# A fused attention, MLP and top-1 mixture-of-experts kernel: routing from raw products, tau loaded elsewhere, and a new order of work around the first expert

## The chip, the cores and the metric

The kernel runs on one core of a Trainium2 chip. The metric is the device time of one execution in microseconds (us); the lower, the better. Engines are named as in the profile: PE is TensorE (PEld its weight loads), DVE is VectorE, ACT is ScalarE, POOL is GpSimd, SP is SyncE, which here only issues DMAs.

## The reference

Three stages run one after the other; the output of each is the input of the next.

```
# attention: batch 4, 8 heads, 576 positions, head size 64, window of 64
scores = where(0 <= i - j < 64, scale * q @ k.T, -1e9)
x = softmax(scores) @ v                       # -> 2304 tokens x 512
# MLP: 512 -> 2048 -> 512
h = x @ w_in;  y = max(0.01 * h, h) @ w_out
# top-1 of 8 experts, 512 -> 1024 -> 512
yn = y / (norm(y) + 1e-6);  en = emb / (norm(emb) + 1e-6)
logits = yn @ en.T / tau
e = argmax(logits);  p = exp(logits - max(logits))
gate = p[e] / (sum(p) + 1e-9)
out = gate * (relu(y @ w1[e]) @ w2[e])
```

## The kernel before

Everything is held in 32-bit floats; the matrix products of the MLP and of the experts are done with each operand split into a high and a low part (three products each), so that every weight tile and every activation tile is first cast to its high part (ACT, sometimes DVE) and then has its low part computed by a subtraction (DVE or POOL).

**Attention** (the first 230 us) goes through 36 chunks of queries. For each, PE transposes q and k (`pq`, `pk`), forms scores `pS` (L344), DVE takes their maximum `mx` (L355), ACT the exponential `sm` (L358), DVE or POOL scales it (`su`, L360 to L362), PE transposes it (`pt`, L380) and multiplies by v (`po`, L396), and ACT and DVE split the result into `xT` (L407, L412). Between these chunks run the first products of the MLP, and the MLP's weights, which come as 64-bit numbers, are turned into 32-bit ones: these conversion pieces are `cv_a` (L189, L190) and `cv_u` (L192, L194) on DVE, L187 and L196 on ACT, L197 on POOL or DVE.

**The MLP** runs in three passes over 16 slices of the hidden layer (4, 4 and 8). A step is a first product `ph` (L537), the leaky ReLU `hs` (ACT L544, DVE L545), its split `gh` (ACT L549, POOL L550), and the second product `acc` (L564), which DVE adds into `ypart` (L575). In the last pass each block of tokens is routed as soon as it is complete (`route`).

**Routing** writes the block's rows to `y_dram`, forms the dot products with the eight normalised expert vectors (on DVE, L654, or for the last two blocks on PE: `py`, `pl`), and the squares of the rows (ACT L643). `sqrt_into` takes the square root by three Newton steps on DVE (L97 to L105), L684 to L686 scale the products by the norm and by tau (`rt`), L688 to L696 find the expert as a one-hot row (`ohf`, `ohb`), L702 to L707 compute the gate. PE counts ranks (`pp<-ohb`, L715), DVE turns them into list positions (`di`, L722 to L730), and POOL scatters token numbers and gates into `list_dram` (L733). Routing is a generator; each `yield "w"` hands control back to the step list of PE.

**The experts.** The expert with the most tokens so far is taken first (`choose_first`), its weights and a first list `ixte` are loaded early, and its tokens are gathered (`prep1`, L899) and transposed (`prep2`, `px` L910, `x2f` L913). The first pair of 128-token tiles (`pair`) computes `ph` (L980) for eight slices: the first four side by side in 48 matmuls, then the rest one after the other, evacuated to `xT` by ACT L983 and DVE L984; then `po` (L956). Work of the last block's routing, the sorting of experts by size (`sort_experts`, L825 to L832), the counting registers (`count_registers`, L842 to L859, result `cnt_i`), the list of the first expert (`load_idx(0, ...)`, L884) and the remaining splits of its weights (`early_split`, L785 high, L786 low) are hung between these matmuls as hooks: hook 0 to 3 after each 12 of the first 48 matmuls, hook 4 after the first two evacuations, hook 5 to 8 after each further slice, and from there after the second products. At hooks 12 to 16 the engines load the counts (`TENSOR_LOAD cnt_i`).

**Order.** On PE everything runs in program order. On DVE, ACT, POOL and SP a scheduler orders the work by priority until the first expert is chosen; from there on their order is the program's too. The conversion pieces have a priority lowered by 100 places, several pieces of the attention a raised one; what stands where in the queues follows from all of these together.

## Time and profile before

| | |
|---|---|
| median of 3 runs | 852.87 us (850.72 to 853.14) |
| profiled execution, its own time | 854.09 us |
| its span in the trace | 852.5 us |
| PE busy | 797.0 us, 93% of the span |
| DVE busy | 541.8 us, 64% |
| ACT busy | 400.4 us, 47% |
| POOL busy | 309.1 us, 36% |
| mean granted clock of PE | 0.984 |

The span is what the trace shows from the first to the last instruction; 1.6 us of the execution's own time lie around it. A busy share is the time in which an engine had an instruction running. The granted clock is the TensorE clock that the chip allowed, as a fraction of the full 2.4 GHz; 0.5 is 1.2 GHz.

### The profile page before, as it was taken

To read this page: it belongs to the slowest core of one execution; us is meant where nothing else is said; L and a number is where in the kernel's file an instruction comes from. 1 tells how busy PE (TensorE), PEld (TensorE's weight loads), DVE (VectorE), ACT (ScalarE), POOL (GpSimd) and SP (SyncE) were. 2 spreads that over 40 slices of the span, in tenths; PEclk is the share of its full clock that TensorE was granted. 3 is DMA by queue.
4 is the path that set the end of the run, shared out by engine and by line. 5 is a ranking of instruction groups with operands and counts; after the bars stand their busy time and mean duration, and the time that the engine had idled before them with its cause. 6 is when DMAs were issued, how large, how long until landed. Compare 5 with 4: busy or idle time off the path is not lost.

```text
span 852.5 us, 13946 instructions
## 1 busy us (share of the span) xinstructions
PE 797.0 (93%) x4864; PEld 712.4 (84%) x4864; DVE 541.8 (64%) x1272; ACT 400.4 (47%) x971; POOL 309.1 (36%) x300
## 2 busy tenths in 40 slices
PE   8688888999999999999999998987899999999994
PEld 6677787888898999999988887876789989889893
DVE  5999698976468222827798899847251166363560
ACT  5787668867554222523323233353342255454551
POOL 2354332232343232342333443452552145244431
PEclk9899999999999999999999999999899999999998
DMA  9668555852256443232203212073681147385610
GB/s 223 173 155 203 115 154 151 231 143 69 60 186 180 124 149 109 90 115 95 89 24 87 51 38 75 27 233 117 200 271 38 38 154 254 142 275 174 210 63 18
DMA packets 101189, 113.01 MB, mean 133 GB/s; under 512 B 61662, under 2 KB 80222, under 8 KB 99568
## 3 DMA queue, kind: packets, MB, share of 16 engines
q1 hardware_dynamic: 87760, 79.42, 31.8%
q0 software_dynamic: 13344, 32.54, 12.4%
q8 instruction: 43, 0.70, 0.3%
q14 instruction: 42, 0.34, 0.1%
HBM read 92.28 MB, written 20.32 MB: 132 GB/s over the span
## 4 chain that ended last, share of the span: by engine, by line
PE 67%; DVE 19%; ACT 5%; issue 4%; DMA 3%; POOL 0%; SPq 0%; POOLq 0%; DVEq 0%; ACTq 0%
PE ph L537 19%; PE acc L564 18%; PE ph L980 10%; PE po L956 9%; DVE jk L654 3%; PE pS L344 2%; DVE xT L412 2%; ACT sm L358 1%; PE po L396 1%; DVE mx L355 1%; DVE sm L354 1%; PE px L910 1%; DVE hs L545 1%; PE pt L380 1%; PE pa L1053 1%
## 5 line engine op out<-in xcount | busy, mean ns | idle before, releaser
L537 PE MATMUL ph<-xT,w 128*128 128x384 f32 (+1 forms) x1344 | 231.8, 318 | 3.1 <-DVE xT L412 3.0
L564 PE MATMUL acc<-w,gh 128*128 128x512 f32 x864 | 222.3, 398 | 5.3 <-POOL gh L550 2.9
L537 PEld LDWEIGHTS ph<-xT,w 128*128 128x128 f32 x1344 | 211.9, 189 | 12.7 <-DVE xT L412 3.9
L550 POOL TENSOR_TENSOR gh<-hs,gh 128x384 fp32r<-128x384 f32 (+1 forms) x112 | 116.1, 1037 | 248.8 <-ACT gh L549 239.0
L564 PEld LDWEIGHTS acc<-w,gh 128*128 128x128 f32 x864 | 157.5, 188 | 35.6 <-POOL gh L550 3.8
L545 DVE TENSOR_TENSOR hs<-ph,hs 128x384 f32<-128x384 f32 (+1 forms) x112 | 55.5, 495 | 100.4 <-ACT hs L544 100.0
L544 ACT ACTIVATE hs<-ph 128x384 f32<-128x384 f32 (+1 forms) x112 | 49.5, 442 | 113.8 <-PE ph L537 107.9
L549 ACT CAST gh<-hs 128x384 fp32r<-128x384 f32 (+1 forms) x112 | 52.3, 467 | 98.7 <-DVE hs L545 98.3
L654 DVE CUSTOM_DVE_ANT_0 jk<-ypart,en_bc 128x512 f32<-128x512 f32 x112 | 84.4, 790 | 0.8 <-ACT sq L643 0.6
L956 PE MATMUL po<-w,hT 128*128 128x512 f32 x312 | 77.1, 396 | 0.0
L956 PEld LDWEIGHTS po<-w,hT 128*128 128x128 f32 x312 | 56.8, 188 | 10.9
L362 POOL TENSOR_TENSOR sm<-sm,su 128x512 f32<-128x512 f32 x36 | 39.8, 1106 | 68.6 <-DVE su L361 50.5
L984 DVE SCALAR_TENSOR_TENSOR hT<-ph,hT 128x512 fp32r<-128x512 f32 x28 | 19.4, 692 | 49.9 <-ACT hT L983 49.9
L980 PE MATMUL ph<-x2f,w 128*128 128x256 f32 x384 | 48.5, 288 | 0.2 <-ACT x2f L912 0.2
L980 PEld LDWEIGHTS ph<-x2f,w 128*128 128x128 f32 x384 | 47.8, 194 | 0.7 <-ACT x2f L912 0.5
L396 PE MATMUL po<-pT,vw 128*128 128x128 f32 x288 | 40.5, 286 | 7.2 <-ACT pT L383 4.7
L344 PE MATMUL pS<-kT,qbd 128*128 128x128 f32 x288 | 43.5, 288 | 3.3 <-ACT sm L358 3.2
L396 PEld LDWEIGHTS po<-pT,vw 128*128 128x128 f32 x288 | 37.8, 198 | 9.5 <-ACT pT L383 5.8
L358 ACT ACTIVATE sm<-sm,mx 128x128 f32<-128x128 f32 x100 | 39.3, 395 | 10.0 <-DVE mx L355 8.1
L344 PEld LDWEIGHTS pS<-kT,qbd 128*128 128x128 f32 x288 | 38.7, 196 | 4.9 <-ACT sm L358 4.0
L786 DVE TENSOR_TENSOR we<-raw,we 128x1024 fp32r<-128x1024 f32 x24 | 34.5, 1451 | 11.4 <-ACT we L785 11.4
L944 POOL DMA_INDIRECT out_dram<-o,ixt x17 | 17.2, 1014 | 65.4 <-ACT o L943 52.5
(233 smaller groups left out, 1252.8 us busy)
## 6 DMA issues: line engine op xcount, KB each, us to landing
raw<-in_moe_w_dram SPq DMA_DIRECT2D x59, 512.0 KB, 5.0
xT<-x_dram POOLq DMA_DIRECT2D x7, 1536.0 KB, 6.8
raw_in<-in_moe_w_in_dram SPq DMA_DIRECT2D x16, 512.0 KB, 3.9
raw_out<-in_moe_w_out_dram SPq DMA_DIRECT2D x16, 512.0 KB, 4.9
xT<-x_dram POOLq DMA_DIRECT2D x7, 1024.0 KB, 6.1
x_dram<-xT SPq DMA_DIRECT2D x4, 1536.0 KB, 5.8
y_dram<-ypart SPq DMA_DIRECT2D x18, 256.0 KB, 2.3
kn<-in_k_dram SPq DMA_DIRECT2D x16, 256.0 KB, 4.6
```

The source lines that it names most:

```text
L344: nc.tensor.matmul(pS[:, pr, :], qbd[b, kt][:, pr, ch, :], keys, start=True, stop=not early)
L358: nc.scalar.activation(s[:, pr, :], src[:, pr, :], AF.Exp, bias=mx[:, pr:pr + 1], scale=1.0, accum_out=su[:, pr:pr + 1])
L396: nc.tensor.matmul(po[:, pr, :], vt[:, 2 * pr:2 * pr + 2, :].rearrange("p h d -> p (h d)"), t[:, pr, :], start=True, stop=True)
L537: nc.tensor.matmul(ph[:, :n], lhs, rhs, start=(cnt == 0), stop=(cnt == 3 * KD - 1))
L544: nc.scalar.mul(hs[:, :n], ph[:, :n], 0.01)
L545: nc.vector.tensor_tensor(out=g[:, :n], in0=ph[:, :n], in1=hs[:, :n], op=ALU.max)
L549: nc.scalar.copy(gh[:, 0, :n], g[:, :n])
L550: nc.gpsimd.tensor_tensor(out=gh[:, 1, :n], in0=g[:, :n], in1=gh[:, 0, :n].bitcast(F32), op=ALU.subtract)
L564: nc.tensor.matmul(a, lhs, rhs, start=(c == 0 and i == 0), stop=(c == PASSES[pas] - 1 and i == 2))
L654: nc.vector.tensor_tensor_reduce(out=jk, in0=y, in1=rp["en"][:, e, :], scale=1.0, scalar=0.0, op0=ALU.mult, op1=ALU.add, accum_out=lg[:, m ...
L956: nc.tensor.matmul(po, lhs, rhs, start=(f == 0 and i == 0), stop=(f == KF - 1 and i == 2))
L980: nc.tensor.matmul(ph, lhs, rhs, start=(kk == 0 and i == 0), stop=(kk == KD - 1 and i == 2))
```

## The change

Seven edits are made at once. `sqrt_into` halves its input once and fuses two operations of each Newton step, 10 instructions in place of 12. The low part of the very last `gh` is computed on DVE, not on POOL. In the last pass the additions into `ypart` get the scheduler's default high priority. Tau is folded into the norm of the expert vectors (before, into the token's norm), and its load is written behind the first weight load. The router finds the maximum and the expert from the raw products and computes the square root, the norm and the gate behind that. `split_expert` is cut into a high and a low part. And the hooks of the first pair are arranged anew.

```diff
@@ sqrt_into
         for it in range(3):
             nc.vector.reciprocal(rc, y)
+            if it == 0:
+                nc.vector.tensor_single_scalar(x, x, 0.5, op=ALU.mult)
             nc.vector.tensor_tensor(out=rc, in0=rc, in1=x, op=ALU.mult)
-            nc.vector.tensor_tensor(out=rc, in0=rc, in1=y, op=ALU.add)
+            nc.vector.scalar_tensor_tensor(out=dst, in0=y, scalar=0.5, in1=rc, op0=ALU.mult, op1=ALU.add)
             y = dst
-            nc.vector.tensor_single_scalar(y, rc, 0.5, op=ALU.mult)
@@ l1, rest()
-                nc.gpsimd.tensor_tensor(out=gh[:, 1, :n], in0=g[:, :n], in1=gh[:, 0, :n].bitcast(F32), op=ALU.subtract)
+                (nc.vector if (pas, t, c) == steps[-1] else nc.gpsimd).tensor_tensor(out=gh[:, 1, :n], in0=g[:, :n], in1=gh[:, 0, :n].bitcast(F32), op=ALU.subtract)
@@ l2
-                with tc.high_priority(offset=PRIO):
+                with tc.high_priority(offset=PRIO if pas < 2 else None):
@@ en_setup
-        nc.vector.tensor_single_scalar(nr, nr, 1e-6, op=ALU.add)
+        nc.vector.tensor_scalar(out=nr, in0=nr, scalar1=1e-6, scalar2=rt[:E], op0=ALU.add, op1=ALU.mult)
...
-        nc.sync.dma_start(out=rt, in_=tau.to_broadcast([P, 1]))
@@ route
             yield "w"
-            if last:
-                squares()
-                sqrt_into(nr, ss, p2, nm)
-            yield "w"
+            if not last:
+                yield "w"
             pl = ps.tile([P, 4, E], F32, name="pl", tag="s")
...
             nc.vector.tensor_copy(lg, pl[:, :nm])
-        if not last:
-            sqrt_into(nr, ss, p2, nm)
-        nc.vector.tensor_scalar(out=nr, in0=nr, scalar1=1e-6, scalar2=rt, op0=ALU.add, op1=ALU.mult)
-        nc.vector.reciprocal(nr, nr)
-        nc.vector.tensor_tensor(out=lg, in0=lg, in1=bc(nr, E), op=ALU.mult)
...
         nc.vector.tensor_copy(ohb, ohf)
+        if last:
+            squares()
+            yield "w"
+        sqrt_into(nr, ss, p2, nm)
+        nc.vector.tensor_single_scalar(nr, nr, 1e-6, op=ALU.add)
+        nc.vector.reciprocal(nr, nr)
         rec = p2.tile([P, 4, 3], I32, name="rec")[:, :nm]
-        if last:
-            yield "w"
...
         nc.vector.tensor_tensor(out=ex, in0=lg, in1=bc(mx, E), op=ALU.subtract)
+        nc.vector.tensor_tensor(out=ex, in0=ex, in1=bc(nr, E), op=ALU.mult)
...
-        for _ in range(4 if t in DVE_DOTS else 2):
+        for _ in range(4 if t in DVE_DOTS else 1 if last else 2):
             yield "w"
@@ the start
     load_w(0)
+    nc.sync.dma_start(out=rt, in_=tau.to_broadcast([P, 1]))
     ensure_v(4)
@@ first pair, hooks
-            0: [step], 1: [step, lambda: early_split((5,))], 2: [lambda: early_split((6,))], 3: [step, step],
-            4: [pump_all, sort_experts, lambda: load_expert(1, range(4)), lambda: early_split((4,))], 6: [lambda: early_split((7,))],
-            7: [count_registers], 11: [lambda: load_idx(0, ixt[0]), lambda: load_idx(1, ixt[1])], 17: [lambda: prep1(0, 2), lambda: prep1(0, 3), lambda: load_expert(1, range(4, 8), nc.gpsimd)],
+            0: [step], 1: [step, step, lambda: early_high(5)], 2: [pump_all, lambda: early_high(6)],
+            4: [lambda: load_idx(0, ixt[0]), lambda: early_low(5), lambda: early_low(6), lambda: early_split((4,))],
+            5: [sort_experts, lambda: load_expert(1, range(4))], 6: [lambda: early_split((7,))],
+            7: [count_registers, lambda: prep1(0, 2), lambda: prep1(0, 3)], 11: [lambda: load_idx(1, ixt[1])], 17: [lambda: load_expert(1, range(4, 8), nc.gpsimd)],
```

`early_high` and `early_low` are the two halves of `early_split` for one weight tile. The tau load stood at the end of `en_setup` in the program, but the scheduler had put it sixth on SP; it now stands behind the loads `raw_in` and `raw_out` of the first weights.

PE's order is unchanged but for `pl` and `pp` of the last block: `pl` now follows 12 of the first pair's matmuls (24 before) and `pp` 36 (48 before). The other engines' orders change in three places that matter.

On DVE in the attention stage, the conversion pieces (`cv_a`, `cv_u`) stand otherwise among the attention's instructions. Before, around the eleventh maximum `mx`:

```order
L412 TENSOR_TENSOR xT<-po,xT 64x4x64 x2
L192 SCALAR_TENSOR_TENSOR cv_u<-raw_out,cv_a 128x512
L360 TENSOR_SCALAR su<-su 128x4
L194 SCALAR_TENSOR_TENSOR cv_u<-raw_out,cv_u 128x512
L361 RECIPROCAL su<-su 128x4
L189 TENSOR_SCALAR cv_a<-cv_a 128x512
L355 TENSOR_REDUCE mx<-pS 128x4
```

And of the change, the last eleven rows up to the same maximum (its line numbers are one higher):

```order
L195 SCALAR_TENSOR_TENSOR cv_u<-raw_out,cv_u 128x512
L190 TENSOR_SCALAR cv_a<-cv_a 128x512 x2
L191 TENSOR_SCALAR cv_a<-cv_a 128x512 x2
L193 SCALAR_TENSOR_TENSOR cv_u<-raw_in,cv_a 128x512
L193 SCALAR_TENSOR_TENSOR cv_u<-raw_out,cv_a 128x512
L195 SCALAR_TENSOR_TENSOR cv_u<-raw_in,cv_u 128x512
L413 TENSOR_TENSOR xT<-po,xT 64x4x64 x2
L195 SCALAR_TENSOR_TENSOR cv_u<-raw_out,cv_u 128x512
L546 TENSOR_TENSOR hs<-ph,hs 128x256
L361 TENSOR_SCALAR su<-su 128x4
L356 TENSOR_REDUCE mx<-pS 128x4
```

The pieces now stand in a clump: sixteen between the tenth maximum and the eleventh, five before. Counted from the start of the queue, 25 conversion pieces stand ahead of the eleventh maximum before and 32 of the change; ahead of the tenth they are 20 and 16, ahead of the fourteenth to eighteenth 39 in both, ahead of the 26th 66 and 70, and from the thirtieth on 84 in both.

On DVE in the routing of the last block, from the copy of the products `lg` on. Before, the square root (L97 to L105) stands ahead of these rows:

```order
L681 COPY lg<-pl 128x16
L684 TENSOR_SCALAR nr<-nr,rt 128x2
L685 RECIPROCAL nr<-nr 128x2
L686 TENSOR_TENSOR lg<-lg,nr 128x16
L688 TENSOR_REDUCE mxl<-lg 128x2
```

Of the change, the one-hot row `ohb`, for which PE's `pp` waits, comes ahead of the square root:

```order
L679 COPY lg<-pl 128x16
L682 TENSOR_REDUCE mxl<-lg 128x2
L685 TENSOR_TENSOR ohf<-lg,mxl 128x16
L686 TENSOR_TENSOR ohf<-ohf,rev_109 128x16
L687 TENSOR_REDUCE ft<-ohf 128x2
L688 TENSOR_TENSOR ohf<-ohf,ft 128x16
L690 CAST ohb<-ohf 128x16
L97 TENSOR_SCALAR sq_i<-ss 128x2
```

The evacuations of the first pair's `ph` stand behind the routing chain and its `di` on DVE in both; the sort (`c_key`) follows `di` at once before, and of the change comes behind five evacuations and one weight split.

On POOL at the first pair: low parts of the weights w1, w2, w5, w6 (rows `w<-raw`), the two scatters into the list, and the gathers of the first expert's next tokens (`ypart<-y_dram`). Before:

```order
L786 TENSOR_TENSOR w_6338<-raw_5_2920,w_6338 128x1024
L786 TENSOR_TENSOR w_6353<-raw_6_2921,w_6353 128x1024
L733 DMA list_dram<-rec,di 18432x3 x2
L791 TENSOR_LOAD c_pi_6429
L1328 TENSOR_LOAD cnt_i x5
L899 DMA ypart<-y_dram,ixt_6148 128x512 x2
```

Of the change:

```order
L732 DMA list_dram<-rec,di 18432x3 x2
L788 TENSOR_TENSOR w_6347<-raw_5_2918,w_6347 128x1024
L788 TENSOR_TENSOR w_6388<-raw_6_2919,w_6388 128x1024
L797 TENSOR_LOAD c_pi_6436
L905 DMA ypart<-y_dram,ixt_6134 128x512 x2
L1342 TENSOR_LOAD cnt_i x5
```

The scatters are now ahead of the low parts of w5 and w6, and the gathers ahead of the count loads.

## Rows read from the trace of the kernel before

**Rows 1.** PE's waits: waiter, whom for: us in total, times, longest.

```profile
PE px L910 <- DMA ypart<-y_dram,ixt: 2.9, 2, 1.4
```

**Rows 2.** Windows, core 0: span, busy us of PE, PEld, DVE, ACT, POOL, clock, DMA.

```profile
20.00:66.00 46.00, 34.81 (x247) 32.05 (x246) 43.33 (x89) 35.57 (x118) 21.68 (x18) 0.89 0.67 174
230.00:555.00 325.00, 321.47 (x1776) 288.60 (x1775) 222.46 (x650) 107.66 (x245) 118.01 (x133) 1.00 0.32 98
```

**Rows 3.** Timeline of DVE, attention: start us, us, line, instruction [idle before].

```profile
51.10 0.69 DVE L355 TENSOR_REDUCE mx<-pS 128x4 f32<-128x512 f32 x1
...
53.31 0.42 DVE L190 TENSOR_SCALAR cv_a<-cv_a 128x512 int32<-128x512 int32 x1
...
55.35 0.69 DVE L192 SCALAR_TENSOR_TENSOR cv_u<-raw_out,cv_a 128x512 int32<-128x512 int32 x1
...
57.43 0.69 DVE L355 TENSOR_REDUCE mx<-pS 128x4 f32<-128x512 f32 x1 [0.26 <-PE pS L346]
```

**Rows 4.** Timeline of PE, attention: the two groups of scores behind those maxima.

```profile
55.54 0.49 PE L344 MATMUL pS<-kT,qbd 128*128 128x128 f32 x2 [2.96 <-ACT sm L358]
...
61.99 1.16 PE L344 MATMUL pS<-kT,qbd 128*128 128x128 f32 x8
```

**Rows 5.** Timeline of SP's queue: the tau load at the start.

```profile
5.29 1.14 SPq L596 DMA_DIRECT2D rt<-in_moe_tau_dram  x1
```

**Rows 6.** Timeline of PE, end of the MLP and first pair.

```profile
565.88 1.20 PE L564 MATMUL acc<-w,gh 128*128 128x512 f32 x4 [2.05 <-POOL gh L550]
...
568.01 0.66 PE L910 MATMUL px<-ident,ypart 128*128 128x128 f32 x4
...
569.34 3.15 PE L980 MATMUL ph<-x2f,w 128*128 128x256 f32 x24 [0.24 <-ACT x2f L912]
572.33 1.84 PE L678 MATMUL pl<-enT,yT 128*128 128x8 f32 x16
...
581.46 0.18 PE L715 MATMUL pp<-ohb,tri 128*128 128x8 bf16 x1 [4.30 <-DVE ohb L696]
...
581.59 7.46 PE L980 MATMUL ph<-x2f,w 128*128 128x256 f32 x48
...
591.48 8.67 PE L956 MATMUL po<-w,xT 128*128 128x512 f32 x36 [0.32 <-DVE c_tmp L851]
...
605.84 13.25 PE L980 MATMUL ph<-x2r,w 128*128 128x256 f32 x96
```

**Rows 7.** DMA issues, 560 to 570 us: count, KB each, us to landing.

```profile
ypart<-y_dram,ixte POOLq DMA_INDIRECT x2, 3.8
```

**Rows 8.** Timeline of DVE, routing of the last block and counts.

```profile
575.06 2.39 DVE L105 TENSOR_SCALAR nr<-sq_r 128x2 f32<-128x2 f32 x1
...
577.48 2.26 DVE L684 TENSOR_SCALAR nr<-nr,rt 128x2 f32<-128x2 f32 x1
...
581.22 0.17 DVE L696 CAST ohb<-ohf 128x16 bf16<-128x16 f32 x1
...
584.39 0.16 DVE L730 SCALAR_TENSOR_TENSOR di<-rl,eo 128x2 int32<-128x2 int32 x1
...
586.29 1.22 DVE L786 TENSOR_TENSOR w<-raw,w 128x1024 fp32r<-128x1024 f32 x1
...
590.72 0.17 DVE L844 CAST cnt_i<-c_num 128x8 int32<-128x8 f32 x1
```

**Rows 9.** Timeline of POOL: low parts of w5 and w6, a scatter, a gather.

```profile
575.02 4.69 POOL L786 TENSOR_TENSOR w<-raw,w 128x1024 fp32r<-128x1024 f32 x2 [4.53 <-ACT w L785]
...
586.17 0.99 POOL L733 DMA_INDIRECT list_dram<-rec,di  x1 [0.31 <-issue]
598.14 1.03 POOL L899 DMA_INDIRECT ypart<-y_dram,ixt  x1 [10.98 <-DMA ixt<-list_dram]
```

**Rows 10.** Windows: both stretches of PE with a low clock.

```profile
581.40:588.90 7.50, 7.45 (x54) 7.45 (x55) 6.71 (x31) 4.45 (x10) 2.02 (x2) 0.77 0.01 2
...
600.10:612.00 11.90, 9.02 (x50) 8.46 (x50) 2.07 (x3) 3.27 (x5) 4.89 (x7) 0.71 0.70 239
```

More of the change, by code (lines that the diff above doesn't have):

```diff
@@ L776, in half_of_first, with split_high @@
         q.dma_start(out=rawt[0][:, sl], in_=w1[bass.ds(regs[0], 1), 0:P, sl].rearrange("o p f -> (o p) f"))
-    def split_expert(par, j, eng=None, dve_hi=False):
-        raw, w = rawt[j], wexp[par, j]
-        hi = w[:, 0:2, :].rearrange("p a d -> p (a d)")
-        lo = w[:, 2:4, :].rearrange("p a d -> p (a d)")
+    def split_high(par, j, dve_hi=False):
+        raw, hi = rawt[j], wexp[par, j][:, 0:2, :].rearrange("p a d -> p (a d)")
         if dve_hi:
@@ L785, in split_expert, with split_low @@
             nc.scalar.copy(hi, raw)
+    def split_low(par, j, eng=None):
+        raw, w = rawt[j], wexp[par, j]
+        hi = w[:, 0:2, :].rearrange("p a d -> p (a d)")
+        lo = w[:, 2:4, :].rearrange("p a d -> p (a d)")
         (eng or nc.vector).tensor_tensor(out=lo, in0=raw, in1=hi.bitcast(F32), op=ALU.subtract)
+    def split_expert(par, j, eng=None, dve_hi=False):
+        split_high(par, j, dve_hi)
+        split_low(par, j, eng)
     sel = {}
@@ L933, in early_prep, with early_high, early_low @@
         load_expert(0, range(1, 3))
+    def early_high(j):
+        wexp[0, j] = wp.tile([P, 4, DM], F32R, name=f"w{j}", tag=f"w{j}")
+        split_high(0, j)
+    def early_low(j):
+        split_low(0, j, nc.gpsimd if j in (1, 2, 5, 6) else nc.vector)
     def early_split(js):
         for j in js:
-            wexp[0, j] = wp.tile([P, 4, DM], F32R, name=f"w{j}", tag=f"w{j}")
-            split_expert(0, j, nc.gpsimd if j in (1, 2, 5, 6) else nc.vector)
+            early_high(j)
+            early_low(j)
     def flush(s, b, po, new_o):
```

## The prediction, made before the changed kernel was run

> **What bounds the kernel now.** I read the busy shares first: PE works 93% of the span and nothing else over 64%, so a gain must come from time in which PE stands still or runs slowly, or from the rest of the span. The list of PE's waits names who is waited for; one entry, the `px` of the first expert, is 2.9 us in two waits [rows 1]. Then windows tell in which stage PE is really the limit: in the MLP it is busy 321.47 of 325 us, in the attention stage from 20 to 66 us only 34.81 of 46, where DVE is busy 43.33 of 46 [rows 2]. So there are two places with anything to win or lose: the attention stage, where DVE sets the pace, and the turn from the MLP to the experts, where the timeline of PE shows the waits one by one (part 2 and on). What is lost in the first is carried through the MLP, which has about 3.5 us of idle PE in 325 us to absorb it with, scattered over small waits.
>
> **The change, part 1: the order on DVE in the attention stage.** The pieces of weight conversion are the same in number and kind, but seven more of them now stand ahead of the eleventh maximum: three of the short kind and four of the long. With 0.42 us for a short one and 0.69 us for a long one [rows 3] that is 3 x 0.42 + 4 x 0.69 = 4.0 us. Is there cover? From the tenth maximum at 51.10 to the scores that waited for it at 55.54 it takes 4.44 us; from the eleventh at 57.43 the same 4.44 us lead to 61.87, and PE takes up those scores at 61.99 [rows 3, 4]. The cover is 0.1 us. So I put the whole 4.0 us on the path. Further on, ahead of the 26th maximum, four more pieces stand than before, one short and three long: 0.42 + 3 x 0.69 = 2.5 us. That the tenth maximum has four pieces fewer ahead of it helps little, since the next one has sixteen. The bounds: nothing, because from the thirtieth maximum on the count of pieces is the same and DVE might make it up in its idle time; and 8 us, if in the clump a POOL pass also blocks DVE once, as it does later for 2.39 us [rows 8] (4.0 + 2.5 + 2.4, less 1.1 of the next sentence). The tau load leaves SP's queue ahead of the third pair of loads; it took 1.14 us there [rows 5], and I count -1.1. Its new place is behind 1 MB of weights and ahead of nothing that is due at once. Part 1 in sum: +4.0 + 2.5 - 1.1 = +5.4, between 0 and +8.
>
> **Part 2: the end of the MLP.** The last low part of `gh` goes to DVE. Before, PE waited 2.05 us for it [rows 6]. But what follows on PE is two `px`, the second at 568.01, and its rows come from a gather on POOL that lands 3.8 us after its issue [rows 6, 7]; `ph` starts at 569.34 from there. The gather isn't moved, so the wait goes over from `acc` to `px`: 0, and at most -1 if the gather is issued earlier. The two instructions fewer in each square root, the priority of the additions into `ypart`, and the extra multiplication `ex` lie on DVE under a PE that hardly waits [rows 2]; they cost or bring nothing (0.2 us each, if that cover went).
>
> **Part 3: routing of the last block.** Per matmul of the first pair, 24 take 572.33 - 569.34 = 2.99 us, 0.125 each [rows 6]. `pl` now follows 12 of them: 570.84, and with 1.70 us of its own (to the next `ph`) it ends at 572.5. From `lg` to `ohb` there are now seven small instructions at 0.2 us: ready at 574.0 (before: 581.22 [rows 8], behind the square root and two scalings that took 2.39 and 2.26 us). PE comes to `pp` after 24 more matmuls at 575.5 and doesn't wait. The wait of 4.30 us [rows 6] is gone, and PE is there with 48 - 36 = 12 matmuls still to make up.
>
> What is late next? On DVE, 14 instructions of norm (2.8 us), one more for the gate, and the 2.5 us from `ohb` to `di` (584.39 - 581.22, less 0.7 for two evacuations) put `di` at about 579.5. Only then come the evacuations of `ph`; PE needs the first of them at 575.5 + 24 x 0.125 = 578.5 and gets it at 580.0: a new wait of 1.5 us. 36 matmuls (4.5 us) and nine `po` (36 take 8.67 us [rows 6], so 2.2) later, at 586.7, PE comes to the count load. The count comes from DVE: after `di` at 579.6 two evacuations (0.7), a split (1.2 [rows 8]), three evacuations (1.1), the sort (584.55 to 586.29, 1.7), evacuation, split, evacuation (2.0) and three instructions (0.6) make 586.9, and from the start of `cnt_i` to PE's go it was 591.48 - 590.72 = 0.8 us: 587.5. That is 4.0 us earlier than before.
>
> But now the low parts of w5 and w6 run on POOL behind the scatters, from about 582.2 (579.6 and two scatters of 0.99 + 0.31 us) to 586.9 (4.69 us for the pair [rows 9]), and the sort on DVE stands beside them. Before, the same pair stood beside the norm: two instructions on two numbers took 2.39 and 2.26 us, one for each pass [rows 8, 9]. If the sort (it begins at 582.6) is held in the same way to 586.9, the count is ready at 586.9 + 1.7 + 2.0 + 0.6 = 591.2, and PE goes on at 591.8 (0.6 from the end of `cnt_i`, 590.89, to 591.48 before): 0.3 later than before, and the whole wait of `pp` is given back. I take this end, because the rows show the same pair of passes blocking small DVE instructions twice in a row. Part 3: +0.3, between -4.0 and +0.3. The Trainium skill says of this, in SBUF — State Buffer, under "Who interferes with whom", that DVE and GpSimd share one pair of ports as an exclusive lock, held for the whole instruction by whichever starts first, and that casts, copies, scalings and operations on two SBUF tensors are the DVE instructions that can be shut out. The 2.39 us of this trace agree. By the rule alone the count would come at 591.2 where POOL starts first, and about 2.3 us sooner where a DVE instruction gets in between the two passes.
>
> **Part 4: the first expert's list.** Its load goes ahead of the sort and of four weight loads, right behind the scatters. Gathers on POOL waited 10.98 us for that list, to 598.14 [rows 9]. Now `di` is 4.9 us earlier and the load no longer waits for the sort (1.7 us): at least 6.6 us. The gathers need less: PE is done with the 36 `po` at 591.48 + 8.67 = 600.2, and the second gather, issued 1.03 + 0.31 us behind the first, landed 3.8 us later [rows 7, 9], at 603.3; 3.1 us are enough. So both `px` waits, 2.9 us [rows 1], fall away. Around them PE ran at half clock: the window from 600.1 to 612 has 0.71 [rows 10], and 96 matmuls took 13.25 us where four times 2.99 are 12.0 [rows 6], 1.2 us, with some more on the few matmuls ahead of them (at most 11.9 x 0.29 = 3.4 in all, if PE had never waited there). I take 1.8. The other low stretch, 0.77 from 581.4 to 588.9 [rows 10], cost 7.46 - 2 x 3.15 = 1.2 us; it came just after PE's idle 4.3 us, and as PE will now be idle for about as long at the count load, I leave it in. Part 4: -4.7, between -2.9 (the second stretch too comes back after the new wait) and -5.9 (both gone).
>
> **Sum.** +5.4 + 0 + 0.3 - 4.7 = +1.0 us. On the profiled execution's own time that is 854.09 + 1.0 = 855.1; the median of the three runs lies 1.2 us lower, so the forecast is 852.87 + 1.0 = 853.9. About 0.3%, 2.6 us, is what a measurement of this kernel can tell from no change.
>
> **Rivals.** *The attention stage absorbs its new order.* DVE has 2.7 us of idle time in 46 there [rows 2] and the totals are equal by the thirtieth maximum; against it speaks the cover of 0.1 us. Then parts 3 and 4 decide: 852.9 + 0.3 - 4.7 = 848.5, or 847.4 with the tau load's 1.1.
>
> *The sort is not held up.* If DVE gets between POOL's passes, or the passes start later than the sort, PE goes on at 587.5 to 589.5 and gains 2.3 to 4.3 us on the sum; the idle time is then some 1 to 2.5 us and the low clock may go as well: 853.9 - 4.3 - 1.2 = 848.4. For it: POOL's two scatters stand ahead; against: POOL took both turns in rows 8.
>
> *Slower: the attention stage costs all it can, and the new idle time keeps PE's clock low.* 8 us there, and the half clock comes after the count load for as long as it did around `px`: 852.9 + 8 + 0.3 - 2.9 = 858.3. With -2.9 for part 4 it decides from +5.2 us in the attention stage on (5.2 + 0.3 - 2.9 = 2.6).
>
> **How the numbers follow.** Forecast as summed (851 to 856.5) 0.42; absorbed 0.24; sort not held up 0.14; slower 0.20. Of the forecast's 0.42 about 0.03 lie below -2.6 us, 0.10 above +2.6; of the two faster rivals 0.04 fall short of it. So faster 0.37, same 0.33, slower 0.30. The range holds 8 in 10 when it takes in the centres of all the rivals: 847 to 859.
>
> **What would show it.** Right: in the changed profile a wait of PE for `sm` or `mx` of over 4 us near 60 us, and the MLP's last matmul 4 to 6 us later than before; no wait of `pp`; a wait of 1 to 2 us of `ph` for an evacuation; PE idle some 4.5 us ahead of the 36 `po`, with DVE's sort stretched beside two POOL passes; no wait of `px<-ident,ypart` behind them. Wrong: PE's `acc` ends no later than before (part 1 fails), or the count load waits under 2 us (part 3), or `px` still waits for its gather (part 4).

## Result, and the profile after

The change takes 864.0 us (median of 5; 860.61 to 864.74) against 853.14 us (median of 5; 850.72 to 854.88): a ratio of 1.0117, interval [1.0093, 1.0141]. The forecast was 853.9 us and its range ended at 859, so the kernel lost 10.9 us where 1.0 was expected. The profiled execution is the quickest of the five: 860.61 us, a span of 858.9 (before: 852.5). Its trace accounts for 6.4 us of the loss. In all, nine executions of the change lie either at 859.8 to 860.6 us (four) or at 864.0 to 864.7 (five), and both that were profiled are of the lower kind.

The head of the changed kernel's page, and its list of PE's waits (waiter, whom for: us in total, times, longest):

```profile
span 858.9 us, 13946 instructions
...
PE 800.0 (93%) x4864; PEld 713.5 (83%) x4864; DVE 537.1 (63%) x1257; ACT 399.5 (47%) x971; POOL 309.6 (36%) x299
```

```profile
PE pt L381 <- DVE qbd L332: 8.0, 4, 3.0
PE pS L345 <- ACT sm L359: 6.2, 3, 3.7
PE po L969 <- DVE c_tmp L857: 5.6, 1, 5.6
...
PE px L916 <- DMA ypart<-y_dram,ixte: 1.7, 2, 1.2
...
PE ph L993 <- DVE xT L997: 1.2, 1, 1.2
```

The wait of `pp` for `ohb` and that of `px` for the first expert's gather [rows 1, 6] are gone; a wait of `po` for the count (`c_tmp`, 5.6 us) stands in their place; and two waits of the attention stage, for `sm` and for `qbd`, are now the largest.

**Where the time went.** PE's order is the same in every kernel here but for `pl` and `pp`, so the start of one and the same instruction can be compared. This table has the starts of nine of the 36 `pt` groups of the attention stage, of each kernel's profiled execution less those of before (us, worked out from the timelines of PE; the experiments are told below):

```
start before      52.0  61.3  66.4 131.6 143.4 153.3 171.2 182.0 227.4
the change        -1.4   2.0   8.2   4.4   7.4   7.1   9.5   9.5   9.4
e10, once more    -1.9   1.2   7.3   3.5   6.5   6.2   8.6   8.6   8.5
e1  tau alone     -1.8   1.5   7.6   3.6   5.3   8.5  10.4  12.0  12.0
e4                -1.5   0.0  -0.3   0.4   0.2   3.2   3.7   3.7   3.7
e5                -0.4   2.4   4.7  -0.1   1.6   4.8   6.7   8.3   8.3
e9                -2.5  -0.2   0.0   0.8   1.3   4.2   5.9   5.9   5.9
e12               -1.6   0.2   5.7   2.2   3.0   3.7   3.7   3.6   3.5
e13               -0.8   1.4   2.5  -0.6   0.1   2.6   2.5   2.4   2.3
e2  late alone    -1.5  -0.2  -0.3  -0.3  -0.3   1.2   0.6   0.6   0.6
e3                -0.9  -0.9  -1.3  -1.3  -1.3   0.2  -0.3  -0.4  -0.3
```

The change jumps by 9.6 us between 52 and 66 us, is given 3.8 back by 131, and loses 5.1 more by 171. The 9.4 us then stand unchanged through the MLP.

Kernels whose attention queues are the same as before (e2, e3, and e7 and e8, which are not shown) scatter from -1.7 to +2.5 us against before, mostly by a jump of 1.5 to 3.0 between 143 and 153 that the profile of before lacks. The traces show what that jump is. PE waits there 1.86 us for `gh` ahead of `pk` in all of them; behind that wait it goes on at full clock before and in e11, and at half clock in e2, e3, e7 and e8. Timeline of PE, before and then e7:

```profile
149.13 0.63 PE L298 MATMUL pk<-ident,kn 128*128 128x128 f32 x4 [1.86 <-ACT gh L549]
```

```profile
148.62 1.08 PE L305 MATMUL pk<-ident,kn 128*128 128x128 f32 x4 [1.86 <-ACT gh L556]
```

And a window behind it, before and then e7 (us; PE, PEld, DVE, ACT, POOL busy; granted clock; DMA):

```profile
150.00:152.00 2.00, 2.00 (x11) 1.62 (x11) 2.00 (x5) 1.81 (x7) 0.19 (x1) 1.00 1.12 381
```

```profile
150.00:152.00 2.00, 2.00 (x7) 1.62 (x7) 2.00 (x5) 2.00 (x8) 0.00 (x0) 0.50 1.07 411
```

So the same order with the same wait can cost up to 3 us more or less here, and a difference of that size in one column says nothing of an order by itself.

The first jump, in the timeline of PE (start us, us, line, instruction [idle before]) of the changed kernel:

```profile
53.51 0.49 PE L345 MATMUL pS<-kT,qbd 128*128 128x128 f32 x2 [2.29 <-ACT sm L359]
...
56.60 0.80 PE L538 MATMUL ph<-xT,w 128*128 128x256 f32 x2 [1.55 <-ACT w L197]
59.02 1.22 PE L538 MATMUL ph<-xT,w 128*128 128x256 f32 x4 [1.62 <-POOL w L198]
60.04 1.91 PE L397 MATMUL po<-pT,vw 128*128 128x128 f32 x8
...
67.68 2.08 PE L345 MATMUL pS<-kT,qbd 128*128 128x128 f32 x8 [3.71 <-ACT sm L359]
69.41 2.91 PE L565 MATMUL acc<-w,gh 128*128 128x512 f32 x6
```

and DVE's in the same stretch, with a POOL row beside them:

```profile
59.00 1.75 DVE L193 SCALAR_TENSOR_TENSOR cv_u<-raw_in,cv_a 128x512 int32<-128x512 int32 x1 [1.15 <-POOL w L198]
...
62.76 0.86 DVE L413 TENSOR_TENSOR xT<-po,xT 64x256 fp32r<-64x256 f32 x2 [0.81 <-ACT xT L408]
...
65.41 0.68 DVE L356 TENSOR_REDUCE mx<-pS 128x4 f32<-128x512 f32 x1
```

```profile
56.63 3.57 POOL L198 TENSOR_TENSOR w<-cv_u,w 128x512 fp32r<-128x512 f32 x2 [4.02 <-ACT w L197]
```

The eleventh maximum starts at 65.41, where it was 57.43 [rows 3]: 8.0 us later. The clump's pieces are not only many. DVE stands idle among them for POOL (1.15 us) and for `xT` (0.81), and one piece, which begins while POOL works on its low parts, takes 1.75 us where such a piece took 0.69 [rows 3]. The 0.81 us go back to PE itself: `xT` is an evacuation of the `po` that starts at 60.04, behind a `ph` that had waited 1.62 us for POOL's low part. The scores behind the maximum start at 67.68, where they were 61.99 [rows 4]: 5.7 later. It is not 8.0, because before, ACT had stood between two of the four exponentials until PE's `po` was there (timeline of ACT before):

```profile
58.58 0.36 ACT L358 ACTIVATE sm<-pS,mx 128x128 f32<-128x128 f32 x1
...
60.36 0.74 ACT L407 CAST xT<-po 64x256 fp32r<-64x256 f32 x2 [1.34 <-PE po L396]
61.13 0.37 ACT L358 ACTIVATE sm<-pS,mx 128x128 f32<-128x128 f32 x1
```

Behind the scores PE is busy at half clock, as these windows show:

```profile
64.00:68.00 4.00, 0.32 (x1) 0.33 (x2) 3.94 (x8) 3.96 (x14) 3.98 (x4) 0.76 0.93 282
68.00:72.00 4.00, 4.00 (x14) 3.52 (x14) 3.85 (x7) 0.79 (x2) 1.64 (x2) 0.50 0.91 153
```

At 0.50 the engine runs at 1.2 GHz. The six `acc` took 2.91 us; before, they took 1.63 (timeline of PE before):

```profile
62.91 1.63 PE L564 MATMUL acc<-w,gh 128*128 128x512 f32 x6
```

By the `pt` of 66.4 the delay has grown from 5.7 to 8.2.

The second half of the loss has another waiter. Timeline of PE, changed kernel, and the same two instructions before:

```profile
143.27 0.63 PE L381 MATMUL pt<-ident,sm 128*128 128x128 f32 x4 [2.35 <-DVE qbd L332]
...
180.65 0.63 PE L381 MATMUL pt<-ident,sm 128*128 128x128 f32 x4 [3.01 <-DVE qbd L332]
```

```profile
137.34 0.63 PE L380 MATMUL pt<-ident,sm 128*128 128x128 f32 x4 [0.86 <-DVE qbd L331]
...
171.18 0.63 PE L380 MATMUL pt<-ident,sm 128*128 128x128 f32 x4 [0.76 <-DVE qbd L331]
```

Here PE waits for `qbd`, the evacuation of the transposed queries, for 2.35 and 3.01 us; before, it was 0.86 and 0.76. What stands ahead of `qbd` on DVE at the second of them:

```profile
177.25 1.15 DVE L289 COPY vw<-vw 64x512 f32<-64x512 f32 x1
178.44 0.69 DVE L193 SCALAR_TENSOR_TENSOR cv_u<-raw_out,cv_a 128x512 int32<-128x512 int32 x1
179.04 0.85 DVE L413 TENSOR_TENSOR xT<-po,xT 64x256 fp32r<-64x256 f32 x2
179.81 0.69 DVE L332 TENSOR_SCALAR qbd<-pq 64x512 f32<-64x512 f32 x1
```

**The late part.** PE from the routing on, changed kernel, to be laid beside [rows 6]:

```profile
584.20 0.18 PE L714 MATMUL pp<-ohb,tri 128*128 128x8 bf16 x1
...
584.33 3.08 PE L993 MATMUL ph<-x2f,w 128*128 128x256 f32 x24
588.59 4.54 PE L993 MATMUL ph<-x2f,w 128*128 128x256 f32 x36 [1.17 <-DVE xT L997]
592.97 2.27 PE L969 MATMUL po<-w,xT 128*128 128x512 f32 x9
600.85 10.72 PE L969 MATMUL po<-w,xT 128*128 128x512 f32 x36 [5.62 <-DVE c_tmp L857]
611.41 1.03 PE L916 MATMUL px<-ident,ypart 128*128 128x128 f32 x8
...
613.17 0.50 PE L993 MATMUL ph<-x2r,w 128*128 128x256 f32 x2
614.00 11.42 PE L993 MATMUL ph<-x2r,w 128*128 128x256 f32 x94 [0.34 <-DVE x2r L919]
```

`pp` comes 2.7 us later than before, where the MLP is 9.4 late: 6.7 us less. Of these, 4.3 are the wait that is gone; 1.5 are no gain, since `pp` now has 12 of the 48 matmuls behind it and not ahead; and 0.7 come from the start of the pair, whose first `ph` is 8.7 us late and not 9.4. The 36 `po` start 9.4 us later than before: the waits for the evacuation and for the count have taken all of it back. DVE and POOL show why:

```profile
591.45 4.73 DVE L831 SCALAR_TENSOR_TENSOR c_key<-cnt,rev 128x8 f32<-128x8 f32 x1
...
600.09 0.17 DVE L850 CAST cnt_i<-c_num 128x8 int32<-128x8 f32 x1
```

```profile
591.42 4.73 POOL L788 TENSOR_TENSOR w<-raw,w 128x1024 fp32r<-128x1024 f32 x2
```

The first instruction of the sort, on 8 numbers a partition, takes 4.73 us, from 0.03 us after POOL begins the low parts of w5 and w6 until both are done. It takes 4.72 to 4.74 us in all seven further profiles that have this pair beside the sort (e2, e4, e5, e9, e10, e12, e13). The Trainium skill (SBUF — State Buffer, "Who interferes with whom") gives the pair of ports that DVE and GpSimd share to whichever begins first, for its whole instruction. The rows above agree that the later one is shut out, for an operation on two tensors in SBUF; but here it was shut out through two POOL instructions on end, where before each of two DVE instructions was held for one pass [rows 8, 9].

Behind that wait the `po` run at half clock for a while: 10.72 us in place of 8.67 [rows 6]. From +9.4 us at their start it is +2.05 for them, -2.9 for the two waits of `px` [rows 1], -1.2 for the few `px` and `po` up to the 96 `ph` (2.8 us without the waits before, 1.6 now), and -1.0 for the 96 `ph` themselves, which take 12.25 us from 613.17 on in place of 13.25 [rows 6]; both now run at full clock. That makes +6.3 us behind the first pair, and +6.4 in the span.

### The profile page after: what moved, and what is told of

Its sections match the earlier page's. It is cut to its first block, busy times and chain, and to the rows that moved or that the text cites. A ratio compares the mean times of both kernels' runs of the same rounds, so it can differ in the third digit from the quotient of the medians.

```text
span 858.9 us, 13946 instructions
## 1 busy us (share of the span) xinstructions
PE 800.0 (93%) x4864; PEld 713.5 (83%) x4864; DVE 537.1 (63%) x1257; ACT 399.5 (47%) x971; POOL 309.6 (36%) x299
## 4 chain that ended last, share of the span: by engine, by line
PE 65%; DVE 15%; ACT 7%; issue 4%; DMA 1%; POOL 1%; POOLq 0%; ACTq 0%; DVEq 0%
PE ph L538 18%; PE acc L565 17%; PE po L969 10%; PE ph L993 10%; DVE jk L654 3%; ACT sm L359 2%; PE pS L345 1%; ACT xT L408 1%; PE po L397 1%; DVE sm L355 1%; PE px L916 1%; DVE mx L356 1%; DVE xT L413 1%; PE pt L381 1%; PE pa L1066 1%
## 5 line engine op out<-in xcount | busy, mean ns | idle before, releaser
L565 PE MATMUL acc<-w,gh 128*128 128x512 f32 x864 | 224.9, 402 | 2.5 <-DVE ypart L576 2.3
L565 PEld LDWEIGHTS acc<-w,gh 128*128 128x128 f32 x864 | 159.6, 191 | 33.0 <-ACT gh L550 2.5
L413 DVE TENSOR_TENSOR xT<-po,xT 64x256 fp32r<-64x256 f32 x72 | 30.3, 421 | 17.2 <-ACT xT L408 16.2
```

The costliest lines, as they stand in the source:

```text
L565: nc.tensor.matmul(a, lhs, rhs, start=(c == 0 and i == 0), stop=(c == PASSES[pas] - 1 and i == 2))
```

## Experiments

Every ratio is to the kernel before, timed on the same chip. First come the runs that split the change in two (e1 to e3), then those on the attention stage (e4 to e6, e9, e12, e13), then those on the late part (e7, e8, e11), and last the change once more (e10).

**e1, tau alone.** The kernel before, with only the tau load moved.

```diff
@@ en_setup
-        nc.sync.dma_start(out=rt, in_=tau.to_broadcast([P, 1]))
@@ the start
     load_w(0)
+    nc.sync.dma_start(out=rt, in_=tau.to_broadcast([P, 1]))
```

> The kernel before, with only the tau load moved behind the first weight loads. Its DVE, ACT and POOL orders in the attention stage become those of the change; the end of the program stays that of before. Theory A (the attention stage's new order carries the whole loss): about 9.5 us slower than before, 862.5, or up to 866 if the further 3 us of most runs of the change come from there too; in the trace the last acc of the MLP ends 9 to 10 us later, pp waits 4.3 us as before. Rival B (the loss comes from routing, the square roots or the first pair): no change, 853.

865.54 us, ratio 1.0144 [1.0116, 1.0172]; before 852.83. One small load, written in another place, costs 12.7 us. By the traces the queues of DVE, ACT and POOL are those of the change up to 108 us; from there to 126 us a few instructions around the square root of the expert vectors stand otherwise (it has its old form here), and behind them, to the end of the attention stage, the order is the change's again. The jumps are the change's too (table). It loses 2.6 us more than the change by 227 us. The wait of the change at 180.65 is here too, as long as there, but with half clock behind it, where the change has 1.00 from 182 to 188 (PE's timeline, then a window):

```profile
181.58 1.08 PE L380 MATMUL pt<-ident,sm 128*128 128x128 f32 x4 [3.00 <-DVE qbd L331]
```

```profile
182.00:188.00 6.00, 6.00 (x35) 5.82 (x34) 4.73 (x11) 2.68 (x8) 1.48 (x2) 0.75 0.31 98
```

**e2, everything but tau.** The change, with the tau load, its folding and the square root of the expert vectors as before, so that the attention stage's queues are those of before.

```diff
@@ en_setup
-        nc.vector.tensor_scalar(out=nr, in0=nr, scalar1=1e-6, scalar2=rt[:E], op0=ALU.add, op1=ALU.mult)
+        nc.vector.tensor_single_scalar(nr, nr, 1e-6, op=ALU.add)
...
+        nc.sync.dma_start(out=rt, in_=tau.to_broadcast([P, 1]))
@@ route
-        nc.vector.tensor_single_scalar(nr, nr, 1e-6, op=ALU.add)
+        nc.vector.tensor_scalar(out=nr, in0=nr, scalar1=1e-6, scalar2=rt, op0=ALU.add, op1=ALU.mult)
@@ the start
-    nc.sync.dma_start(out=rt, in_=tau.to_broadcast([P, 1]))
```

> All edits of the change but those that reach the attention stage: tau is loaded and used as before (in the token's norm), the expert vectors' square root keeps its old form, so that every queue up to the last pass is that of before. Theory A: the late part alone gains about 3 us, 850; the wait of pp (4.3) and those of px (2.9) are gone, and a wait of 5 to 6 us stands ahead of the 36 po. Rival B (the late part loses): 853 or more.

851.81 us, ratio 0.9983 [0.9963, 1.0003]. The late edits are worth about 1 us, not told apart from none; about 3 were expected. PE's marks in the profiles show 3.6 us from the MLP to the end of the first pair (+0.6 to -3.0), against one profile of before, whose execution was 1.2 us over its median. e1 and e2 together, +12.7 - 1.0 = +11.7, make up the change's +10.9.

**e3, and no POOL beside the sort.** e2, with the low parts of w5 and w6 on DVE, ahead of and behind the sort.

```diff
-        split_low(0, j, nc.gpsimd if j in (1, 2, 5, 6) else nc.vector)
+        split_low(0, j, nc.gpsimd if j in (1, 2) else nc.vector)
...
-            4: [lambda: load_idx(0, ixt[0]), lambda: early_low(5), lambda: early_low(6), lambda: early_split((4,))],
+            4: [lambda: load_idx(0, ixt[0]), lambda: early_split((4,)), lambda: early_low(5)],
...
-            7: [count_registers, lambda: prep1(0, 2), lambda: prep1(0, 3)], ...
+            7: [count_registers, lambda: early_low(6), lambda: prep1(0, 2), lambda: prep1(0, 3)], ...
```

> As the late part alone, with the low parts of w5 and w6 on DVE, w5 before the sort and w6 behind the counts, so that no POOL pass runs beside the sort. Theory A (the sort's first instruction is shut out by the two POOL passes for 4.7 us): the wait ahead of the 36 po falls from 5.6 to about 2 us, the two DVE splits cost 1.2 us each, 3 us better than the late part alone, 847. Rival C (the count is late because DVE has too much ahead of it, whatever POOL does): the wait stays over 4 us, time as the late part alone or slower.

850.63 us, ratio 0.997 [0.9951, 0.9989]: the fastest median of the study, ahead of both kernels, though only 1.2 us from e2 where 3 were expected. Without the POOL pair the sort is not held (DVE's timeline, then PE's waits):

```profile
583.65 0.16 DVE L838 SCALAR_TENSOR_TENSOR c_key<-cnt,rev 128x8 f32<-128x8 f32 x1
```

```profile
PE po L976 <- DVE c_tmp L864: 2.2, 1, 2.2
...
PE po L976 <- DVE w L795: 0.8, 1, 0.8
```

The same instruction takes 0.16 us, and the wait for the count is 2.2 us in place of 5.6. Of the 3.4 us 0.8 come back as a wait for the low part that DVE now computes, and as much again because the half clock, which sets in here too, finds PE at work: the 36 `po` end 12.4 us after their start, 10.7 in e2.

**e4, tau's place left to the scheduler.** The change, with the tau load in `en_setup` ahead of the sum of squares.

```diff
@@ en_setup
+        nc.sync.dma_start(out=rt, in_=tau.to_broadcast([P, 1]))
         nc.vector.tensor_tensor_reduce(out=sq, in0=e8, in1=e8, scale=1.0, ...
@@ the start
-    nc.sync.dma_start(out=rt, in_=tau.to_broadcast([P, 1]))
```

> All edits of the change, but the tau load is written where the expert vectors are prepared and the scheduler places it, as before. This gives a third order of DVE, ACT and POOL in the attention stage, neither that of before nor that of the change. Theory A (what counts is the order on DVE, which any edit ahead of it can turn): the attention stage ends within 2 us of before and the whole takes 848 to 851. Rival D (folding tau into the expert vectors, or the shorter square root, costs in that stage): 860 or more, as the change.

853.96 us, ratio 1.0007 [0.9989, 1.0025]. With tau folded as in the change, but loaded where the scheduler likes, the first jump is gone (-0.3 at 66.4) and 10 of the 10.9 us with it: the loss comes with the place of the load (by the order that it brings, as e9 and e13 show below), not with the folding. The expectation was missed by 2 us all the same. DVE's queue is that of before up to 108 us and another one from there on, and the attention stage ends 3.7 us late; 3.0 of these lie between 143 and 153, where e7, with the queues of before, has the same 3.0.

**e6, tau at the end of the hand-written part,** just ahead of `man.close()`, and the low parts as in e3.

```diff
     conv_pump(20)
+    nc.sync.dma_start(out=rt, in_=tau.to_broadcast([P, 1]))
     conv_q.append(conv_gen(1))
     man.close()
```

> All edits of the change, but the tau load stands at the end of the hand-ordered stretch, some 50 instructions later, and w5 and w6 have their low parts on DVE. A fourth order in the attention stage, with no clump like that of the change. Theory A: the attention stage ends within 3 us of before, and with 2 us from the late part 848 to 853. Rival D (folding tau or the shorter square root costs in that stage): 858 or more.

853.69 us, ratio 1.001 [0.9997, 1.0024]: no first jump either (-1.0 at 66.4), +2.0 at 227, and a time just over the expected range. A load written by hand is not the trouble in itself.

**e5, no POOL among the conversion pieces.** The change, with the conversion's low parts (`w<-cv_u,w`) of the first four slices on DVE.

```diff
-LOWDVE = 4
+LOWDVE = 0
```

> The change, with the low parts of the first weights' conversion on DVE and not on POOL (8 instructions). Theory A with its second half (the clump of conversion pieces costs twice its own length because pieces in it wait for POOL's low parts and are held up beside them): the waits of PE near 57 to 68 us shrink by 3 us or more although DVE gets 7 us more work, 858 to 861. Rival E (only the number of pieces ahead of the maximum counts): DVE has more to do, so the time is that of the change or worse, 864 to 870.

858.83 us, ratio 1.0068 [1.0044, 1.0091]. The first jump is 5.1 us (from -0.4 to 4.7) in place of 9.6, the loss after 131 us is 8.4 in place of 5.0. That agrees with POOL's passes being part of the price of the clump, but doesn't show it: e5 moves the order as well. Between the tenth maximum and the eleventh DVE now has ten pieces (eight of the kinds counted in the change, and two low parts) where the change has sixteen. What POOL costs in the clump is read from the change's own rows: 1.15 us of idle time and 1.06 us of a longer piece.

**e9, the clump split.** The change, with maximum and exponential of the attention raised by 20 places.

```diff
-APRIO = 0
+APRIO = 20
```

> The change, with one constant of the scheduler turned (the attention's steps rank 20 places higher). Tau's load, the folded tau and the square root stay as in the change; on DVE the eleventh maximum now stands in the middle of the clump, behind 24 conversion pieces and not 32, and the 26th behind 62 and not 70. Theory A (what costs is the clump ahead of the maximum): the jump of 6 us or more of PE near 60 to 68 us goes down to 2 at most and the whole to 855 to 859. Rival D (tau's place or the folding costs in that stage): 864 as the change.

858.5 us, ratio 1.0062 [1.0047, 1.0078]. The first jump is smaller and ends level with before (from -2.5 to 0.0 at 66.4), with tau's load where the change has it: it is the order that costs, not the load. The second half, from 0.8 to 5.9, is as large as in the change, although only 62 conversion pieces stand ahead of the 26th maximum (70 in the change, 66 before). So the pieces ahead of that maximum don't seem to be what costs there; but 2.9 of e9's 5.1 us lie between 143 and 153, where unchanged queues show up to 3.0, and its waits are others than the change's. Two of e9's waits of PE in that half:

```profile
151.75 0.66 PE L299 MATMUL pk<-ident,kn 128*128 128x128 f32 x4 [3.20 <-ACT qbd L329]
...
170.18 0.63 PE L381 MATMUL pt<-ident,sm 128*128 128x128 f32 x4 [1.85 <-ACT kT L303]
```

**e12, the queries first.** The change, with the transposes of q and k and their evacuations raised further.

```diff
@@ tr_step
-            with tc.high_priority(offset=PRIO):
+            with tc.high_priority(offset=80):
```

> The change, with the evacuations of the transposed q and k (qbd, kT) ranked 35 places higher by the scheduler. The clump ahead of the eleventh maximum stays (32 pieces), the seventeenth qbd stands behind 76 pieces and not 79. Theory J (the second half of the attention stage loses because qbd comes late on DVE behind pieces and xT): the jumps of PE between 130 and 182 us, 5 us in the change, fall to 2 or less, the first jump stays at 6 or more, in all 3 us better than the change. Rival K (the second half loses because DVE and ACT have come out of step with PE in the first, whatever the order there): jumps of 4 us or more remain, time as the change.

855.2 us, ratio 1.0035 [1.002, 1.0049]; before 853.75. The first jump stays (+5.5 from 61.3 to 66.4); from 131 to 171 it loses 1.5 where the change loses 5.1. The two halves are separate, and the second one hangs on the evacuations that were raised, `qbd` above all by the two waits below (`kT` was raised with it). The gain is larger than expected: against before, e12 is 9.4 us better than the change by the medians, 5.9 by the marks at 227, and its twelve executions make one group. PE's timeline of e12, the two waits of above:

```profile
140.36 0.63 PE L381 MATMUL pt<-ident,sm 128*128 128x128 f32 x4 [1.71 <-DVE qbd L332]
...
174.83 0.63 PE L381 MATMUL pt<-ident,sm 128*128 128x128 f32 x4 [0.34 <-DVE qbd L332]
```

**e13, both.** `APRIO = 20` and the offset of 80 together.

> Both: the clump split at the eleventh maximum and qbd and kT ranked higher. Theory J with theory A: both jumps shrink, the attention stage ends within 3 us of before and the whole takes 851 to 855. Rival K: the second half still costs 4 us or more, 858.

855.05 us, ratio 1.0018 [1.0003, 1.0034]. Both jumps are small (2.5 at 66.4, 2.3 at 227), but the median is no better than e12's. Of the change's 10.9 us 1.3 are left, with tau's load, the folding and the square root as in the change.

**e7, the list late again.** e3, with the first expert's list loaded at hook 11 and its gathers at hook 17, as before.

```diff
-            4: [lambda: load_idx(0, ixt[0]), lambda: early_split((4,)), ...
+            4: [lambda: early_split((4,)), ...
-            7: [count_registers, lambda: early_low(6), lambda: prep1(0, 2), lambda: prep1(0, 3)], 11: [lambda: load_idx(1, ixt[1])], ...
+            7: [count_registers, lambda: early_low(6)], 11: [lambda: load_idx(0, ixt[0]), lambda: load_idx(1, ixt[1])], 17: [lambda: prep1(0, 2), lambda: prep1(0, 3), ...
```

> As the late part with the lows on DVE, but the first expert's list and its gathers stand behind the counts again, as before. Theory A (the early list takes away the px waits and the half clock around them): px waits about 1.5 to 3 us again, and the time is 2 to 4 us over that of the late part with the lows on DVE, 853 to 854.5. Rival F (the list's place is hidden): same time, 850.6.

852.25 us, ratio 0.9988 [0.9975, 1.0002], 1.6 us above e3 and between the two expectations; the intervals overlap. POOL still waits for the list, PE hardly does (timelines of POOL and of PE):

```profile
599.15 1.04 POOL L912 DMA_INDIRECT ypart<-y_dram,ixt  x1 [14.87 <-DMA ixt<-list_dram]
```

```profile
604.14 0.66 PE L923 MATMUL px<-ident,ypart 128*128 128x128 f32 x4 [0.26 <-DMA ypart<-y_dram,ixt]
```

Without the earlier list the wait of `px` is 0.26 us, not 2.9. Counted from the end of the MLP, the gathers start 0.9 us earlier than before and PE is through with its 36 `po` 1.2 us later, since these now wait for a low part and run at half clock for a while (13.0 us in place of 8.67 [rows 6]).

**e8, `gh` on POOL.** e3, with the last low part of `gh` on POOL as before.

```diff
-                (nc.vector if (pas, t, c) == steps[-1] else nc.gpsimd).tensor_tensor(out=gh[:, 1, :n], ...
+                nc.gpsimd.tensor_tensor(out=gh[:, 1, :n], ...
```

> As the late part with the lows on DVE, but the last low part of gh on POOL again. Theory A (the wait only goes over from acc to px): acc waits about 2 us for gh, px no longer waits for its first gather, the first pair starts within 0.5 us of the other, same time, 850.6. Rival G (gh on DVE is worth its 2 us): 852.5.

850.75 us, ratio 0.9983 [0.9967, 0.9999]: 0.1 us from e3 by the medians, and the intervals overlap. `acc` waits again, `px` for its gather no longer (PE's waits):

```profile
PE acc L571 <- POOL gh L557: 2.3, 2, 2.1
```

**e11, one slice less on POOL.** e3 with `LOWDVE = 3`.

> As the late part with the lows on DVE, and the conversion's low parts of the fourth weight slice moved from POOL to DVE too, a fifth order in the attention stage. It is tried as a faster version. Theory A gives no sign of its own here: DVE has 2 more instructions, POOL 2 fewer; 849 to 853. If it is under 849.5 it is the fastest so far.

851.32 us, ratio 0.9979 [0.9964, 0.9994]: not faster than e3.

**e10, the change once more,** for a profile of an execution of the 864 us kind.

> The change once more, for a second profile of it beside the first, whose time was 860.6 with the other four executions at 864 to 864.7. Theory H (the further 3 us are one more stretch of PE at half clock behind one of the same waits, as in the run with tau alone, whose trace has one at 181 us): PE's marks agree with the first profile to 1 us but for a jump of 1.5 to 3.5 us at one wait with a clock of 0.7 to 0.8 behind it. Rival I (a wait is longer): the jump is there with the clock at 1.0.

859.79, 860.05, 860.20 and 864.73 us; the profiled one is 859.79. Inconclusive: no profile of the upper kind was had.

## Why the prediction was wrong

**Part 1 failed, in its size.** The mechanism was the right one: e1 has its order alone and pays 12.7 us, e4 and e6 do without the order and pay about 1 us, and e13 keeps the load's place, turns the order and pays 1.3. The step that failed is "So I put the whole 4.0 us on the path", with the bounds of 0 and 8 around it:

- *The price of the clump.* Pieces were counted at their undisturbed durations, 4.0 us. The maximum came 8.0 us later, because the clump holds waits of its own: for POOL's low parts, for the drawn-out piece beside a POOL pass, for `xT`. Read off the rows, these are 3.0 of the 4.0 us that the count leaves over. The prediction had POOL's share as 2.4 us in the upper bound only.
- *The cover.* It was taken as 0.1 us since 4.44 us led from either maximum to its scores. From 65.41 to 67.68 it is only 2.27: before, ACT had done two of the four exponentials and then stood behind a `po`, so the 4.44 us were no fixed way. So some 2.3 of the 8.0 us were hidden, and PE got 5.7.
- *The half clock behind the wait* was left out of part 1, though it was counted in part 4. It added 2.5 us at once (5.7 to 8.2). Against that, 3.8 us of the first jump were given back by 131 us, which the sum had not either.
- *The second half* was priced at 2.5 us for four pieces ahead of the 26th maximum. It measures 5.1. In the change's rows what waits is `qbd`, which stands behind other work on DVE, and e12, which ranks `qbd` and `kT` higher, brings it down to 1.5. The prediction watched the maxima alone.
- *Tau's -1.1 us.* No run shows it. SP's queue is level again at the fourth load behind (8.89 us, before 8.90), and PE's 1.4 us ahead at 52 us are not tau's: e2 and e4, with the load at its old place on SP, are 1.5 ahead there too.

**Part 2 was right:** 0 forecast; e8 shows 0.1 us by the medians, and the first pair of the change starts 0.7 us earlier relative to the MLP, inside the bound of -1. The wait moves from `acc` to `px`.

**Part 3 was right,** with its steps: no wait of `pp`; a new wait of `ph` for its evacuation of 1.17 us (forecast: 1.5); the sort held by the POOL pair for 4.73 us; and PE at the 36 `po` no earlier than before, 0.0 us relative to the MLP (forecast: +0.3). e3 takes the pair away and shows the rival "the sort is not held up": 2.2 us of wait are left.

**Part 4 was half right.** The `px` waits, 2.9 us, went, but e7 keeps the list late and waits only 0.26 us, partly because PE comes later. Of the 1.8 us for the half clock nothing stayed over: it went from behind the `px` (-2.2) and came back on the 36 `po` (+2.05). The step that failed here is "I leave it in": the old half-clock stretch stood ahead of the count load, where the wait for the count swallows what its end saves (there 24 matmuls take 3.08 us now, where 48 took 7.46 [rows 6]), while the new one stands behind it, on the path. The value was -4.7; the sum measured from the 36 `po` on is -3.1, near the bound of -2.9.

By the profiles, then, the change is +9.4 - 0.0 - 3.1 = +6.3, of which the forecast had +5.4, +0.3 and -4.7. The rival "slower", with 8 us in the attention stage and a half clock that stays, was the nearest, and its 8 was still too little.

**What stays open.** The medians differ by 10.9 us, the profiles by 6.4. The median of the change is of the 864 us kind, of which there is no profile. The record has the mean granted clock of each execution, though: 0.977 to 0.978 for the four of the lower kind, 0.974 for all five of the upper. A longer wait at full clock would not lower it; 0.0035 of 862 us is 6 us more at half clock, which, as an estimate, costs 3 us where PE is busy throughout, of the 4.2 us between the means of the two kinds. So more half clock fits; which wait it stands behind is not shown. e1's stretch behind the wait at 181.58 is one candidate. The profiles' +6.3 compares single executions, and the traces show that half clock alone moves such a sum by up to 3 us. Nor do the runs show how the scheduler comes from one load's place to that order.

## What to carry to other kernels

When a small edit goes into a part that a scheduler orders, compare the queues of every engine first, and price a new order by the path through all the waiting engines (evacuations as well as reductions), with the waits inside the clump and the half clock that PE may show behind a new wait. Where the late and the early part of a change can be separated, measure them apart: here one is worth 1 to 2 us and the other costs 12.7. A wait taken away ahead of a join is worth what the join's other arm allows; look for that arm (here the count, behind a POOL pair) before counting the gain.

## What was not expected of the hardware

A DVE instruction on 128 x 8 numbers took 4.73 us, through both of two POOL instructions that stood back to back (0.16 us without them, e3): it did not get in between. Beside such a pair before, two DVE instructions on 128 x 2 numbers took 2.39 and 2.26 us, one pass each [rows 8, 9], and in e1 one took 2.25. Those that came through after one pass are TENSOR_SCALAR, with one tensor, and the one that waited for both passes is SCALAR_TENSOR_TENSOR, with two; whether that decides is not shown. And PE's half clock does not follow from a wait alone: behind the same 1.86 us at `pk` PE went on at full clock before and in e11 and at half clock in e2, e3, e7 and e8. Where it could be read, it cost 1.2 to 3.0 us: 1.2 on the 48 `ph` before [rows 6], 1.5 in e2 and 3.0 in e7 at that `pk`, 2.5 behind the 3.71 us wait at 67.68, 2.05 behind the 5.62 us wait at 600.85.
